# Stacking two half-height coefficient blocks of a fused Fourier-mixing and SwiGLU kernel in the 128 partitions, on one Trainium2 core

## The chip, the cores and the metric

The kernel runs on one core of one Trainium2 chip. The metric is the device time of one execution in microseconds (us). The profile's span is about 2 us shorter than the device time of the same execution. PE is TensorE, PEld its weight loads, DVE VectorE, ACT ScalarE, POOL GpSimd, SP the queue that issues most DMAs.

## The reference

```python
def _attn_ref(x):                        # x: 8 x 3008 x 256, float32
    X = np.fft.fft(x, axis=1)
    X = np.fft.fft(X, axis=2)
    return X.real.astype(np.float32)

def _moe_ref(x, w_gate, w_val, w_out):   # 24064 tokens, 256 -> 1536 -> 256
    g = x @ w_gate
    silu = g * (1.0 / (1.0 + np.exp(-g)))
    val = x @ w_val
    return (silu * val @ w_out).astype(np.float32)
```

## The kernel before

The real part of the Fourier transform has mirror symmetries. The kernel folds each batch's 3008 rows down to one eighth, 188 for the odd sums and 188 for the even sums, multiplies by cosine and sine tables on TensorE, and merges the 256-point transform along the features into the weights. Each 188 are one chunk of 128 rows ("A", the long chunk) and one short chunk ("C") of 60 rows, to which, for the even sums, the row for input row 0 is added. Two batches share the 128 partitions of a short chunk, one in each half.

Each batch has two transform jobs: one for the outputs 4i and 4i+2 (`part == 0`, "4i/4i+2 job"), one for 4i+1 (`part == 1`, "4i+1 job"). A job runs twice, once for each of two operands of the feed-forward part (`eo`, called halves here: `eo=0` fills `Pt`, `eo=1` fills `Qt`), and each half has an odd sum in a PSUM buffer of pool `v` and an even sum in one of pool `g`. ACT copies the odd sum to SBUF (`od`), DVE then adds and subtracts the two into `Pt` or `Qt`. The rest is the feed-forward network: 24 tiles of up to 512 columns, each in 12 units of 128 hidden features. A job is issued between two units, and the units use the same PSUM pools of three buffers each.

```python
psG = ctx.enter_context(tc.tile_pool(name="psG", bufs=3, space=bass.MemoryType.PSUM))
psV = ctx.enter_context(tc.tile_pool(name="psV", bufs=3, space=bass.MemoryType.PSUM))
psO = ctx.enter_context(tc.tile_pool(name="psO", bufs=2, space=bass.MemoryType.PSUM))
# ...
def blocks(b, q):
    p0 = 64 * (b % 2)
    return [(0, slice(0, P), *coef_a(b)), (1, slice(p0, p0 + 64) if b else slice(0, P), *coef_c(b))]

def row0(b, q, ps):
    for ch, r, CE, BB in blocks(b, q):
        for kind, cols in ((0, slice(0, GH + 1)), (1, slice(GH + 1, NCE))):
            nc.tensor.matmul(ps[0:1, cols], CE[r, q, 0, kind, P:P + 1], Tab[r, ch, q, 0, cols],
                             start=False, stop=True, skip_group_check=True)

def transform(b, part, eos, given=None):
    # ...
    for q, pool, nm in ((0, psV, "v"), (1, psG, "g")):
        # ... ps = one buffer for each eo, blk = blocks(b, q)
        for j, (ch, r, CE, BB) in enumerate(blk):
            tab = Tab[r, ch, q]
            for eo in eos:
                for kind in range(2):
                    if part == 0:
                        cols = slice(0, GH + 1) if kind == 0 else slice(GH + 1, NCE)
                        l, r_ = CE[r, q, eo, kind, 0:P], tab[:, eo, cols]
                    else:
                        cols = slice(0, G)
                        l = BB[r, q, eo, kind, 0:P]
                        r_ = tab[:, (eo + kind) % 2, NOO:NTAB]
                    nc.tensor.matmul(ps[eo][:, cols], l, r_, ...)
        if part == 0 and 1 in eos and not given:
            row0(b, q, ps[1])
        for eo in eos:
            if q == 0:
                ods[eo] = odp.tile([P, NCE], F32, name="od")
                nc.scalar.copy(ods[eo][:, 0:n], ps[eo][:, 0:n])
            else:
                ev[eo] = ps[eo]
    # ... DVE: Pt or Qt pieces = ev + od or ev - od

def whole_part(b, part):
    transform(b, part, (0,))
    transform(b, part, (1,))
# ... in the loop over units, after part_a(u) and part_b(prev):
        if i in job_at:
            whole_part(*job_at[i])
```

## Time and profile before

| | before |
|---|---|
| device time, median of 4 runs | 673.07 us (672.6 to 673.18) |
| PE, DVE, ACT, POOL busy share of the span | 98%, 82%, 65%, 63% |
| one 4i/4i+2 job, first matmul to the next unit's first | 3.245 us (first half 1.16) |
| one 4i+1 job, the same | 3.376 us (first half 1.68) |

The page of the kernel before, its span, its first line of busy times (us, share of the span, number of instructions) and the chain of waits, that is the chain of work that ended last, by engine and by line of the kernel:

```profile
span 670.8 us, 12888 instructions
...
PE 656.5 (98%) x4269; PEld 411.6 (61%) x4336; DVE 549.4 (82%) x957; ACT 433.5 (65%) x764; POOL 423.8 (63%) x455
...
PE 94%; DVE 2%; DMA 2%; issue 1%; POOL 1%; ACT 0%; DVEq 0%; ACTq 0%; POOLq 0%
PE o L683 37%; PE g L723 16%; PE v L723 14%; PE g L753 9%; PE v L755 5%; PE v L765 4%; PE g L573 3%; PE v L573 3%; DMA W<-in_moe_w_val_dram 2%; PE g L862 1%; PE v L549 1%; PE g L549 1%; PE o L434 1%; DVE hp L744 0%; DVE hm L768 0%
```

TensorE bounds it. But "98% busy" does not say how well TensorE is used: a matmul's record includes its pipeline latency, so records overlap. A 512-column matmul has a record of 0.38 us and the next one starts 0.217 us later. The Trainium skill says the same of the metric ("Trainium Kernel Development and Optimization", Performance Expectations: matmul busy time is a bad metric, because matmuls are pipelined). What must be read are the distances between starts, called the pitch here: 0.217 us for 512 columns, 0.108 for 256, 0.159 for 376, 0.081 for 189, where nothing disturbs the stream.

The PE timeline of the kernel before, one 4i+1 job (columns: start, duration, engine, line, operation, out<-in, rows*weight columns, shape of the moving operand, how many merged):

```profile
195.71 0.48 PE L573 MATMUL v<-Tab,BBa 128*128 128x376 bf16 x2
196.12 0.49 PE L573 MATMUL v<-Tab,BBc 64*128 64x376 bf16 x2
196.54 0.49 PE L573 MATMUL g<-Tab,BBa 128*128 128x376 bf16 x2
196.97 0.49 PE L573 MATMUL g<-Tab,BBc 64*128 64x376 bf16 x2
197.39 0.49 PE L573 MATMUL v<-Tab,BBa 128*128 128x376 bf16 x2
197.82 0.49 PE L573 MATMUL v<-Tab,BBc 64*128 64x376 bf16 x2
198.24 0.49 PE L573 MATMUL g<-Tab,BBa 128*128 128x376 bf16 x2
198.66 0.49 PE L573 MATMUL g<-Tab,BBc 64*128 64x376 bf16 x2
199.09 0.39 PE L723 MATMUL g<-Pt,Wp 128*128 128x512 bf16 x1
```

A pair should take 2 x 0.159 = 0.32 us, but pairs start 0.41 to 0.43 us apart. The pairs alternate between 128 rows (`128*128`) and 64 rows (`64*128`). The weight loads of the same stretch show what is late:

```profile
195.60 0.21 PEld L573 LDWEIGHTS <-BBa 128*128 128x128 bf16 x2
196.12 0.11 PEld L573 LDWEIGHTS <-BBc 64*128 64x128 bf16 x2 [0.31 <-issue]
196.54 0.11 PEld L573 LDWEIGHTS <-BBa 128*128 128x128 bf16 x2 [0.31 <-issue]
```

Each line merges the two loads of a pair. The first load for 128 rows started at 195.60, 0.11 us before its matmul and under the one before. The first load after a change of the row count starts only with its own matmul (196.12, 196.54), so it is hidden under nothing. From one matmul's start to the next a change takes about 0.255 us instead of 0.159. How much of this is waiting before the load, and how much the load that nothing hides, the records do not separate.

Two events: in the timeline of ACT the copy of the odd sum in a 4i/4i+2 job that started at 167.94; in the timeline of DVE, for the 4i+1 job above, the last step of the unit before (`hp`).

```profile
168.57 0.47 ACT L581 COPY od<-v 128x377 f32<-128x377 f32 x1 [0.43 <-PE v L573]
```

```profile
196.15 0.68 DVE L763 TENSOR_TENSOR hp<-sp,v 128x512 bf16<-128x512 f32 x1
```

The second half's first `v` matmul of that 4i/4i+2 job started at 169.10, just after the copy's end at 169.04.

### The profile page before, as it was taken

To read this page: it belongs to the slowest core of one execution; us is meant where nothing else is said; L and a number is where in the kernel's file an instruction comes from. 1 tells how busy PE (TensorE), PEld (TensorE's weight loads), DVE (VectorE), ACT (ScalarE), POOL (GpSimd) and SP (SyncE) were. 2 spreads that over 40 slices of the span, in tenths; PEclk is the share of its full clock that TensorE was granted. 3 is DMA by queue.
4 is the path that set the end of the run, shared out by engine and by line. 5 is a ranking of instruction groups with operands and counts; after the bars stand their busy time and mean duration, and the time that the engine had idled before them with its cause. 6 is when DMAs were issued, how large, how long until landed. Compare 5 with 4: busy or idle time off the path is not lost.

```text
span 670.8 us, 12888 instructions
## 1 busy us (share of the span) xinstructions
PE 656.5 (98%) x4269; PEld 411.6 (61%) x4336; DVE 549.4 (82%) x957; ACT 433.5 (65%) x764; POOL 423.8 (63%) x455
## 2 busy tenths in 40 slices
PE   8889999999999999999999999999999999999997
PEld 5446666666656666565665666655665656656676
DVE  8796667888888888888888888888888888889962
ACT  8576566666566576575665666656666657666663
POOL 8895953687676787776675767667576333435510
PEclk9999999999999999999999999999999999999999
DMA  9856355335215213344143111125111011111112
GB/s 217 121 76 124 111 127 136 89 92 143 61 33 136 69 50 107 90 98 104 36 109 97 48 33 48 40 68 129 48 41 41 33 44 36 48 32 48 48 48 72
DMA packets 45564, 52.53 MB, mean 78 GB/s; under 512 B 6290, under 2 KB 33466, under 8 KB 45498
## 3 DMA queue, kind: packets, MB, share of 16 engines
q1 hardware_dynamic: 42314, 49.35, 28.0%
q0 software_dynamic: 3184, 2.36, 3.0%
q8 instruction: 34, 0.56, 0.4%
q14 instruction: 32, 0.26, 0.1%
HBM read 29.39 MB, written 24.65 MB: 81 GB/s over the span
## 4 chain that ended last, share of the span: by engine, by line
PE 94%; DVE 2%; DMA 2%; issue 1%; POOL 1%; ACT 0%; DVEq 0%; ACTq 0%; POOLq 0%
PE o L683 37%; PE g L723 16%; PE v L723 14%; PE g L753 9%; PE v L755 5%; PE v L765 4%; PE g L573 3%; PE v L573 3%; DMA W<-in_moe_w_val_dram 2%; PE g L862 1%; PE v L549 1%; PE g L549 1%; PE o L434 1%; DVE hp L744 0%; DVE hm L768 0%
## 5 line engine op out<-in xcount | busy, mean ns | idle before, releaser
L762 POOL TENSOR_TENSOR hm<-sgv,vv 128x512 bf16<-128x512 f32 (+1 forms) x164 | 208.3, 1271 | 190.2 <-DVE vv L758 180.9
L683 PE MATMUL o<-Wo,hp 128*128 128x256 bf16 (+2 forms) x1140 | 169.7, 273 | 0.0
L683 PE MATMUL o<-Wo,hm 128*128 128x256 bf16 (+2 forms) x1140 | 169.7, 273 | 0.0
L683 PEld LDWEIGHTS <-hp 128*128 128x128 bf16 (+2 forms) x1140 | 112.2, 99 | 69.3
L683 PEld LDWEIGHTS <-hm 128*128 128x128 bf16 (+2 forms) x1140 | 112.0, 98 | 69.2 <-issue 0.2
L733 ACT ACTIVATE sp<-g 128x512 f32<-128x512 f32 (+1 forms) x164 | 98.0, 597 | 73.6 <-PE g L723 48.6
L735 DVE SCALAR_TENSOR_TENSOR es<-bc,w,v 128x512 f32<-128x512 f32 (+1 forms) x164 | 121.8, 743 | 5.9 <-PE v L723 5.1
L758 DVE SCALAR_TENSOR_TENSOR vv<-es,v 128x512 f32<-128x512 f32 (+1 forms) x164 | 112.6, 686 | 13.7 <-PE v L755 10.3
L761 ACT ACTIVATE sgv<-g 128x512 f32<-128x512 f32 (+1 forms) x164 | 98.2, 599 | 39.1 <-PE g L753 39.1
L768 DVE TENSOR_TENSOR hm<-sg,v 128x512 bf16<-128x512 f32 (+2 forms) x124 | 82.3, 663 | 41.7 <-ACT sg L767 32.3
L763 DVE TENSOR_TENSOR hp<-sp,v 128x512 bf16<-128x512 f32 (+1 forms) x164 | 111.3, 679 | 0.0
L723 PE MATMUL v<-Pt,Wp 128*128 128x512 bf16 (+2 forms) x288 | 107.9, 375 | 3.4
L723 PE MATMUL g<-Pt,Wp 128*128 128x512 bf16 (+2 forms) x288 | 108.0, 375 | 0.0
L753 PE MATMUL g<-Qt,Wm 128*128 128x512 bf16 (+2 forms) x288 | 107.9, 375 | 0.0
L744 DVE TENSOR_TENSOR hp<-sg,v 128x512 bf16<-128x512 f32 (+2 forms) x124 | 82.4, 664 | 26.6 <-ACT sg L743 24.8
L743 ACT ACTIVATE sg<-g 128x512 f32<-128x512 f32 (+2 forms) x124 | 71.9, 580 | 36.1 <-PE g L723 26.9
L767 ACT ACTIVATE sg<-g 128x512 f32<-128x512 f32 (+2 forms) x124 | 71.9, 580 | 32.5 <-PE g L753 32.3
L723 PE MATMUL g<-Qt,Wq 128*128 128x512 bf16 (+2 forms) x223 | 83.3, 373 | 0.5 <-DVE Qt L586 0.5
L723 PEld LDWEIGHTS <-Wp 128*128 128x128 bf16 x576 | 56.3, 98 | 40.9 <-issue 4.2
L755 PE MATMUL v<-Qt,Wq 128*128 128x512 bf16 (+1 forms) x164 | 62.1, 378 | 0.0
L689 ACT COPY ev<-o 128x512 f32<-128x512 f32 x90 | 52.8, 587 | 7.9 <-PE o L683 7.0
L723 PEld LDWEIGHTS <-Wq 128*128 128x128 bf16 x412 | 40.3, 98 | 19.9 <-issue 0.3
(165 smaller groups left out, 631.2 us busy)
## 6 DMA issues: line engine op xcount, KB each, us to landing
out_dram<-ev SPq DMA_DIRECT2D x96, 128.0 KB
XA<-in_x_dram SPq DMA_DIRECT2D x32, 256.0 KB
XA<-in_x_dram SPq DMA_DIRECT2D x112, 64.0 KB
XC<-in_x_dram SPq DMA_DIRECT2D x32, 120.0 KB
XC<-in_x_dram SPq DMA_DIRECT2D x105, 32.0 KB
out_dram<-ev SPq DMA_DIRECT2D x12, 120.0 KB
out_dram<-ev SPq DMA_DIRECT2D x10, 112.0 KB
XA<-in_x_dram SPq DMA_DIRECT2D x1, 1024.0 KB
```

Of the source, the lines that this page charges most:

```text
L683: nc.tensor.matmul(ps[:n, j, :], hts[minus][:, f, c:c + n], Wo[:, f, :], start=(f == 0), stop=(f == nF - 1))
L723: nc.tensor.matmul(ps[:, :w], Wt[:, gv, fs], src[:, :w], start=start, stop=stop, skip_group_check=True)
L733: nc.scalar.activation(sg[:, :w], g[:, :w], AF.Silu)
L735: nc.vector.scalar_tensor_tensor(es[:, :w], bc[t][:, :w], w0[:, f:f + 1], v[:, :w], op0=Alu.mult, op1=Alu.add)
L744: nc.vector.tensor_tensor(hts[t][0][:, f, :w], sg[:, :w], v[:, :w], op=Alu.mult)
L753: nc.tensor.matmul(g[:, :w], Wm[:, 0, fs], Qt[:, :w], start=False, stop=True, skip_group_check=True)
L755: nc.tensor.matmul(v[:, :w], Wq[:, 1, fs], Qt[:, :w], start=False, stop=True, skip_group_check=True)
L758: nc.vector.scalar_tensor_tensor(vm[:, w - 1::-1], es[:, :w], 2.0, v[:, :w], op0=Alu.mult, op1=Alu.subtract)
L761: nc.scalar.activation(sm[:, w - 1::-1], g[:, :w], AF.Silu)
L762: nc.gpsimd.tensor_tensor(hts[t][1][:, f, :w], sm[:, :w], vm[:, :w], op=Alu.mult)
L763: nc.vector.tensor_tensor(hts[t][0][:, f, :w], sp[:, :w], v[:, :w], op=Alu.mult)
L768: nc.vector.tensor_tensor(hts[t][1][:, f, w - 1::-1], sg[:, :w], v[:, :w], op=Alu.mult)
```

## The change

Intent: do not let the short chunk run at half height. After POOL has folded a short chunk, small SBUF-to-SBUF DMAs put one batch's two kinds of coefficients (4i and 4i+2, and the two kinds of 4i+1) in the two halves of the partitions of a stack tile `St`. In the 4i/4i+2 job each half must meet only its own columns, so the other half of the table is zero; in the 4i+1 job the table is swapped in the upper half. One matmul of 128 rows then replaces two of 64, for batches 1 to 7. The broadcast row `bc` becomes bf16 and one scratch tile shrinks, to make room.

```diff
+    def spread_c(b, F):
+        for half, b_ in ((0, b), (1, b + 1)) if b > 1 else ((1, b),):
+            for kind in range(2):
+                nc.sync.dma_start(out=stack(b_)[64 * kind:64 * kind + 64, :], in_=F[64 * half:64 * half + 64, kind])
 ...
+    def products(b, part, q, eo):
+        CE, BB = coef_a(b)
+        if part == 0:
+            return ([(CE[:, q, eo, k, 0:P], Tab[:, 0, q, eo, e], e) for k, e in ((0, E0), (1, E1))] +
+                    [(stack_of(b, 0)[:, q, eo, 0:P], Tab[:, 1, q, eo, 0:NCE], slice(0, NCE))])
+        res = [(BB[:, q, eo, k, 0:P], Tab[:, 0, q, (eo + k) % 2, NOO:NTAB], slice(0, G)) for k in range(2)]
+        if b:
+            return res + [(stack_of(b, 1)[:, q, eo, :], Tab[:, 0:2, q, eo, NCE:NCE + GH], slice(0, G))]
 ...   (batch 0 as before; row0 likewise: one stack matmul for two)
+    def halve_tables():
+        nc.gpsimd.memset(Tab[0:64, 1, :, :, GH + 1:NCE], 0.0)
+        nc.gpsimd.memset(Tab[64:P, 1, :, :, 0:GH + 1], 0.0)
+    def odd_table(c, half):
+        r = slice(64 * half, 64 * half + 64)
+        src = Tab[r, 1, :, :, NOO + GH * c:NOO + GH * (c + 1)]
+        nc.vector.tensor_copy(Tab[r, c, :, :, NCE:NCE + GH], src[:, :, ::-1] if half else src)
+    before[17] = before.get(17, []) + [halve_tables]
+    for i in range(4):
+        before[13 + i] = [lambda i=i: odd_table(i // 2, i % 2)]
 ...
-            bc[t] = bcp.tile([P, T], F32, name="bc")
+            bc[t] = bcp.tile([P, T], BF16, name="bc")
```

More of the change, by code (lines that the diff above doesn't have):

```diff
@@ L58 @@
     t0 = [sum(wide[:t]) for t in range(nT)]
+    R2 = 4 * G
     NCE = 2 * GH + 1
@@ L75 @@
     cp = ctx.enter_context(tc.tile_pool(name="coef", bufs=2))
+    fcp = ctx.enter_context(tc.tile_pool(name="fc", bufs=1))
+    stp = ctx.enter_context(tc.tile_pool(name="st", bufs=3))
     pqp = ctx.enter_context(tc.tile_pool(name="pq", bufs=5))
@@ L99 @@
     XC = const.tile([P, 8, 2, D], F32, name="XC")
-    SDf = const.tile([P, 2, 4, D], F32, name="SDf")
+    SDf = const.tile([P, R2 // D + 1, D], F32, name="SDf")
     EOf = const.tile([P, 2, 4, P + 1], F32, name="EOf")
@@ L148, in fold_steps @@
         tt = eng.tensor_tensor
-        F = SDf[r, q]
+        F = SDf[r, 0:4]
         E, O = EOf[r, 0], EOf[r, 1]
@@ L178, in quarter_rows @@
         tt(B_[:, 1, :, 0:1], E[:, 3::-3, P:P + 1], E[:, 1:3, P:P + 1], op=Alu.subtract)
-    coefA, coefC = {}, {}
+    coefA, stacks = {}, {}
+    NE = P + 1
+    ND = NE + P
     def coef_a(b):
@@ L186, in coef_a, with stack, stack_of @@
         return coefA[b]
-    def coef_c(b):
-        p = b if b < 2 else 1 + b // 2
-        if p not in coefC:
-            coefC[p] = (cp.tile([P, 2, 2, 2, P + 1], BF16, name="CEc"),
-                        cp.tile([P, 2, 2, 2, P], BF16, name="BBc"))
-        return coefC[p]
+    def stack(b):
+        if b not in stacks:
+            stacks[b] = stp.tile([P, 4 * ND], BF16, name="St")
+        return stacks[b]
+    def stack_of(b, part):
+        S4 = stack(b).rearrange("p (q e n) -> p q e n", q=2, e=2)
+        return S4[:, :, :, 0:NE] if part == 0 else S4[:, :, :, NE:ND]
+    def spread_c(b, F):
+        for half, b_ in ((0, b), (1, b + 1)) if b > 1 else ((1, b),):
+            for kind in range(2):
+                nc.sync.dma_start(out=stack(b_)[64 * kind:64 * kind + 64, :], in_=F[64 * half:64 * half + 64, kind])
     tmp_ctx = ExitStack()
@@ L334 @@
     CEa, BBa = coef_a(0)
-    CEc, BBc = coef_c(0)
+    CEc = tp.tile([P, 2, 1, 2, 1], BF16, name="CEc")
+    BBc = stack(0)[:, 0:8 * P].rearrange("p (q e k d) -> p q e k d", q=2, e=2, k=2)
     ti = [tp.tile([P, 2, NCE], I32, name=f"t1{ch}") for ch in range(2)]
@@ L403, in heads @@
     def heads(eng, ev, od, CE):
-        eng.tensor_tensor(CE[:, :, 0, 0, P:P + 1], ev, od, op=Alu.add)
-        eng.tensor_tensor(CE[:, :, 0, 1, P:P + 1], ev, od, op=Alu.subtract)
+        eng.tensor_tensor(CE[:, :, 0, 0, -1:], ev, od, op=Alu.add)
+        eng.tensor_tensor(CE[:, :, 0, 1, -1:], ev, od, op=Alu.subtract)
     acc = [[None, None], [None, None]]
@@ L539 @@
     last = (pl[:, w_last:w_last + B], ql[:, w_last:w_last + B])
-    def blocks(b, q):
-        p0 = 64 * (b % 2)
-        return [(0, slice(0, P), *coef_a(b)), (1, slice(p0, p0 + 64) if b else slice(0, P), *coef_c(b))]
+    E0, E1 = slice(0, GH + 1), slice(GH + 1, NCE)
     def row0(b, q, ps):
-        for ch, r, CE, BB in blocks(b, q):
-            for kind, cols in ((0, slice(0, GH + 1)), (1, slice(GH + 1, NCE))):
-                nc.tensor.matmul(ps[0:1, cols], CE[r, q, 0, kind, P:P + 1], Tab[r, ch, q, 0, cols],
-                                 start=False, stop=True, skip_group_check=True)
+        CE = coef_a(b)[0]
+        todo = [(CE[:, q, 0, k, P:P + 1], Tab[:, 0, q, 0, e], e) for k, e in ((0, E0), (1, E1))]
+        if b:
+            todo.append((stack_of(b, 0)[:, q, 0, P:P + 1], Tab[:, 1, q, 0, 0:NCE], slice(0, NCE)))
+        else:
+            todo += [(CEc[:, q, 0, k, 0:1], Tab[:, 1, q, 0, e], e) for k, e in ((0, E0), (1, E1))]
+        for l, r_, cols in todo:
+            nc.tensor.matmul(ps[0:1, cols], l, r_, start=False, stop=True, skip_group_check=True)
+    def products(b, part, q, eo):
[4 more added lines that the diff above has]
+        res = [(BB[:, q, eo, k, 0:P], Tab[:, 0, q, (eo + k) % 2, NOO:NTAB], slice(0, G)) for k in range(2)]
+        if b:
+            return res + [(stack_of(b, 1)[:, q, eo, :], Tab[:, 0:2, q, eo, NCE:NCE + GH], slice(0, G))]
+        return res + [(BBc[:, q, eo, k, :], Tab[:, 1, q, (eo + k) % 2, NOO:NTAB], slice(0, G)) for k in range(2)]
     def transform(b, part, eos, given=None):
@@ L557, in transform @@
                 ps = {eo: given[eo][q] for eo in eos}
-                blk = []
             else:
                 ps = {eo: pool.tile([P, T], F32, name=nm) for eo in eos}
-                blk = blocks(b, q)
-            for j, (ch, r, CE, BB) in enumerate(blk):
-                tab = Tab[r, ch, q]
                 for eo in eos:
-                    for kind in range(2):
-                        if part == 0:
-                            cols = slice(0, GH + 1) if kind == 0 else slice(GH + 1, NCE)
-                            l, r_ = CE[r, q, eo, kind, 0:P], tab[:, eo, cols]
-                        else:
-                            cols = slice(0, G)
-                            l = BB[r, q, eo, kind, 0:P]
-                            r_ = tab[:, (eo + kind) % 2, NOO:NTAB]
-                        nc.tensor.matmul(ps[eo][:, cols], l, r_, start=(j == 0 and kind == 0),
-                                         stop=(j == len(blk) - 1 and kind == 1), skip_group_check=True)
+                    mms = products(b, part, q, eo)
+                    for i, (l, r_, cols) in enumerate(mms):
+                        nc.tensor.matmul(ps[eo][:, cols], l, r_, start=(i == 0), stop=(i == len(mms) - 1),
+                                         skip_group_check=True)
             if part == 0 and 1 in eos and not given:
@@ L790 @@
     act_at = {}
+    spread_at = {}
+    foldC = {}
     def run_loads(n):
@@ L805, in fold_step @@
             else:
-                queue[what] = fold_steps(nc.gpsimd, XC, *coef_c(b), q, slice(64 if b == 1 else 0, P))
+                if q == 0:
+                    foldC[b] = fcp.tile([P, 2, 4 * ND], BF16, name="Fc")
+                F5 = foldC[b].rearrange("p k (q e n) -> p q e k n", q=2, e=2)
+                queue[what] = fold_steps(nc.gpsimd, XC, F5[..., 0:NE], F5[..., NE:ND], q,
+                                         slice(64 if b == 1 else 0, P))
         queue[what].pop(0)()
@@ L809, in fold_step @@
             act_at.setdefault(max(unit + 2, 11), []).append(what)
+        if kind == "C" and q == 1 and j == 5:
+            spread_at[unit + 2] = b
     def load_next(what):
@@ L836, in weight_unit @@
         return [lambda k=k: weights(fc, gv, k) for k in range(2)]
-    raO = SDf.rearrange("p k a d -> p (k a d)")[:, 0:4 * G].rearrange("p (c q n) -> p c q n", c=2, q=2)
+    raO = SDf.rearrange("p a d -> p (a d)")[:, 0:4 * G].rearrange("p (c q n) -> p c q n", c=2, q=2)
     def angles_o(ch):
@@ L884 @@
             load_next(what)
+        if i in spread_at:
+            spread_c(spread_at[i], foldC[spread_at[i]])
         if i in job_at:
```

## The prediction

> **What bounds it now.** TensorE. The profile page has PE 98% busy, DVE 82%, ACT 65%, POOL 63%; the chain of waits is 94% PE; PE waits sum to a few us. Matmuls follow at a fixed pitch in the timeline: 0.217 us for 512 columns, 0.108 for 256, 0.159 for 376, 0.081 for 189. PE time taken out counts, unless a PSUM buffer is not free.
>
> **What the change removes.** For batches 1 to 7 the short chunk's matmuls use 64 of 128 rows: two per product, two per row-0 sum. Stacked, each pair becomes one 128-row matmul. Per batch (timeline, b=1):
> - 4i+1 job: 16 matmuls of 376 columns take 3.38 us to the next unit (16 x 0.159 would be 2.54): each of 8 changes between 128-row and 64-row matmuls has a pitch of 0.25 us: the next weight load starts only when the stream is done. The Trainium skill, "TensorEngine Tiling (Array Packing)", Key Properties, says that changing tiling mode drains the TensorE; the trace agrees, about 0.095 us a change. After: 12 x 0.159 = 1.90. Saves 1.47.
> - 4i/4i+2 job: 3.24 us, 24 matmuls. After: first half 2 x (2 x 0.081 + 0.159) = 0.64; the second adds row 0 and four mode changes (one weight column): 1.67. Total 2.31. Saves 0.93.
> Sum 2.4 us x 7 = 16.8 us of PE (2.5%).
>
> **What it adds.** 14 SBUF-to-SBUF DMAs of 128 KB, issued two units after the fold and needed many units later; four DVE table copies and two POOL memsets in units 13 to 17, where DVE is 64% busy; POOL folds keep count and size (0.64 us a quarter-row step). bc in bf16 leaves ACT and DVE durations about alone. All this I expect off the chain.
>
> **How much is on the path.** PE now reaches the transforms' PSUM buffers sooner than ACT and DVE free them.
> - 4i/4i+2 job: the second half's v takes the bank that ACT's od copy of the first half has read; already now (7 of 7) it starts 0.05 us after that copy. The copy can begin only 0.1 us sooner, so the first half saves about 0.1, not 0.42. The second saves its 0.42. About 0.5 per batch.
> - 4i+1 job: the second half's v waits for DVE's hp of the previous unit, which ends 0.4 to 0.7 us before now, while PE would come 0.74 sooner; the next unit's g waits for DVE's Pt sums. Laid out with the trace's durations, next g starts about 1.0 us sooner instead of 1.47.
> Sum 1.5 x 7 = 10.6 us; the other 6 become PE waits in or just after the transforms.
>
> **Prediction: 662.5 us, range 658.5 to 667.** Faster by over 2% (below 659.7): 0.18. Within 2%: 0.80. Slower by over 2%: 0.02.
>
> **What would show it.** Stack matmuls of 128 rows with 0.16 us pitch, no 0.25 us steps inside the 4i+1 job; that job near 2.35 us and the 4i/4i+2 job near 2.75 including waits; PE waits on od copies, hp and Pt sums that are not there now; stack DMAs landing long before use; DVE busy the same within 3 us; span outside the transforms unchanged.
>
> **What would make it wrong.** Faster: the buffer waits being shorter (then up to 656). Slower: stack DMAs or their waits on the SP queue delaying output stores and x loads; POOL folds slower with the new layout; DVE backlog growing after each transform, since DVE needs about 2.1 us for a split unit against PE's 1.95.

## The result, and the profile after

The changed kernel takes 662.56 us (median of 4 runs, 662.1 to 662.89), against 673.07 of before. The ratio is 0.9845, with a 95% interval of 0.9828 to 0.9862. Ratios here are the mean time of one kernel's fast runs over that of the other's of the same rounds, so not quite the ratio of the medians quoted. By a threshold of 2% that counts as the same; it is 1.5% faster, clear of noise.

The page of the changed kernel, the lines that answer to those shown of before:

```profile
span 661.1 us, 12780 instructions
...
PE 644.8 (98%) x4199; PEld 413.5 (63%) x4266; DVE 550.4 (83%) x961; ACT 433.3 (66%) x764; POOL 425.5 (64%) x457
...
PE 93%; DVE 2%; DMA 1%; ACT 1%; issue 1%; SPq 0%; POOL 0%; DVEq 0%; ACTq 0%
PE o L697 37%; PE g L737 16%; PE v L737 14%; PE g L767 9%; PE v L769 5%; PE v L779 4%; PE v L587 2%; PE g L587 1%; DMA XA<-in_x_dram 1%; PE v L438 1%; PE g L438 1%; DVE Pt L600 1%; PE g L897 1%; DVE hp L758 1%; ACT od L595 1%
```

PE's share of the span is still 98%, so that number shows nothing of a 10 us gain. In the chain, two entries from the transforms are new: DVE's `Pt` sums and ACT's `od` copy, 1% each.

The PE timeline of the changed kernel, the same 4i+1 job:

```profile
194.22 0.48 PE L587 MATMUL v<-Tab,BBa 128*128 128x376 bf16 x2
194.54 0.33 PE L587 MATMUL v<-Tab,St 128*128 128x376 bf16 x1
194.70 0.48 PE L587 MATMUL g<-Tab,BBa 128*128 128x376 bf16 x2
195.02 0.33 PE L587 MATMUL g<-Tab,St 128*128 128x376 bf16 x1
195.40 0.48 PE L587 MATMUL v<-Tab,BBa 128*128 128x376 bf16 x2
195.72 0.32 PE L587 MATMUL v<-Tab,St 128*128 128x376 bf16 x1
195.88 0.48 PE L587 MATMUL g<-Tab,BBa 128*128 128x376 bf16 x2
196.20 0.32 PE L587 MATMUL g<-Tab,St 128*128 128x376 bf16 x1
196.58 0.38 PE L737 MATMUL g<-Pt,Wp 128*128 128x512 bf16 x1
```

Inside a half every matmul now has the undisturbed pitch (0.32 for two, 0.16 for one). Two gaps are left. From the last stack matmul of the first half (195.02) to the second half (195.40) it is 0.38 us instead of 0.16, and from 196.20 to the next unit (196.58) again 0.38. DVE's timeline has their ends:

```profile
194.67 0.68 DVE L777 TENSOR_TENSOR hp<-sp,v 128x512 bf16<-128x512 f32 x1
195.45 1.07 DVE L600 TENSOR_TENSOR Pt<-g,od 128x272 bf16<-128x272 f32 x3
```

`hp` ends at 195.35, and `v` starts at 195.40. The `Pt` sums end at 196.52, and the next unit's `g` starts at 196.58. Of the two waits only the second sets the length of the job: over batches 1 to 7 the second half starts anywhere from 1.18 to 1.37 us after the first (after `hp` in six of them, after the `od` copy in batch 1), yet all seven jobs take 2.352 to 2.354 us, and in all seven the next `g` starts 0.05 us after the last `Pt` sum. The 4i/4i+2 job of the same batch, its end of the first half and start of the second:

```profile
167.29 0.33 PE L587 MATMUL g<-Tab,CEa 128*128 128x189 bf16 x2
167.46 0.32 PE L587 MATMUL g<-Tab,St 128*128 128x377 bf16 x1
168.02 0.33 PE L587 MATMUL v<-Tab,CEa 128*128 128x189 bf16 x2 [0.24 <-ACT od L595]
```

The first half could have ended at 167.62 (167.46 + 0.16), and the second starts at 168.02, when the `od` copy is done. The view of the waits of PE has this once per batch (us in total, times, longest); the kernel before has no such line:

```profile
PE v L587 <- ACT od L595: 1.6, 7, 0.2
```

It gives 1.6 us in all, though 7 starts came 0.40 us late, 2.8 us in all. The idle time of PE counts only what the modelled ends of the matmuls leave uncovered, and the pipeline latency covers the rest. It lists nothing at all for the `Pt` sums, although they held up each 4i+1 job. Such waits have to be read from the pitch.

The job times from the trace, batches 1 to 7 (range over the seven jobs), and the gain of all seven together:

| job | before | after | undisturbed stream, worked out from the pitches | gain |
|---|---|---|---|---|
| 4i/4i+2 | 3.243 to 3.249 us | 2.733 to 2.738 | 2.31 | 3.6 us |
| 4i+1 | 3.374 to 3.377 us | 2.352 to 2.354 | 1.90 | 7.2 us |

Outside the jobs nothing moved: the stretches between two jobs (from batch 2's first job on) take 24.52, 49.03 and 48.81 us in both kernels. The sum of gains is 10.7 us. In the two profiles 0.6 us of it is missing, because the set-up ended later in the second (over the profiles the first matmul of the main loop starts anywhere from 24.9 to 26.6 us), and 0.5 us more, because the end of the program came 0.5 us later after the last store was issued. In all profiles the last store is issued 11.02 us after the start of the last unit's first matmul; the end comes at 14.25 us before, at 14.78 in the changed kernel, at 13.97 with the stack DMAs doubled (e5 below). The cause is open.

### The profile page after: what moved, and what is told of

It is laid out like the page before. It is cut to its first block, busy times and chain, and to the rows that moved or that the text cites. A ratio compares the mean times of both kernels' runs of the same rounds, so it can differ in the third digit from the quotient of the medians.

```text
span 661.1 us, 12780 instructions
## 1 busy us (share of the span) xinstructions
PE 644.8 (98%) x4199; PEld 413.5 (63%) x4266; DVE 550.4 (83%) x961; ACT 433.3 (66%) x764; POOL 425.5 (64%) x457
## 4 chain that ended last, share of the span: by engine, by line
PE 93%; DVE 2%; DMA 1%; ACT 1%; issue 1%; SPq 0%; POOL 0%; DVEq 0%; ACTq 0%
PE o L697 37%; PE g L737 16%; PE v L737 14%; PE g L767 9%; PE v L769 5%; PE v L779 4%; PE v L587 2%; PE g L587 1%; DMA XA<-in_x_dram 1%; PE v L438 1%; PE g L438 1%; DVE Pt L600 1%; PE g L897 1%; DVE hp L758 1%; ACT od L595 1%
## 5 line engine op out<-in xcount | busy, mean ns | idle before, releaser
L749 DVE SCALAR_TENSOR_TENSOR es<-bc,w,v 128x512 f32<-128x512 bf16 (+1 forms) x164 | 121.8, 742 | 5.6 <-PE v L737 5.3
```

The source lines that it names most:

```text
L749: nc.vector.scalar_tensor_tensor(es[:, :w], bc[t][:, :w], w0[:, f:f + 1], v[:, :w], op0=Alu.mult, op1=Alu.add)
```

## The experiments

All versions but e3 and e6, which are wrong, compute the right result. The first four share a chip and the runs of the kernel before (median 673.15 us), the next four too (672.06 us), and the last has its own (672.95 us).

### e1_halves_apart: the changed kernel, the halves of a job in two units

```diff
-        if i in job_at:
-            whole_part(*job_at[i])
+        if i - 1 in job_at:
+            transform(*job_at[i - 1], (1,))
+        if i in job_at:
+            transform(*job_at[i], (0,))
```

> The changed kernel, with the two halves of each transform job issued in two successive units instead of back to back. Theory (about 6 us of the 16.8 us of PE time is lost waiting for PSUM buffers between the halves and after the second): the waits fall into other work, so 656 to 657.5 us, ratio to before 0.975 to 0.977, with each half near its stream time (0.64 and 1.68 us for the 4i/4i+2 job, 0.95 and 0.95 for the 4i+1 job). Rival A (the missing 6 us is in the matmul stream itself, for example weight loads from the stack that cannot be prefetched, or lost elsewhere): 662 to 663 us, as the changed kernel.

Measured: 656.78 us (655.92 to 656.99), ratio 0.9763 (0.9748 to 0.9777). The halves of the 4i/4i+2 jobs take 0.65 and 1.69 us, those of the 4i+1 jobs 0.96 and 0.96; the unit between them takes 1.95 us in batches 2 to 7, as elsewhere. The first half of a 4i+1 job in its PE timeline:

```profile
191.82 0.48 PE L587 MATMUL v<-Tab,BBa 128*128 128x376 bf16 x2
192.14 0.32 PE L587 MATMUL v<-Tab,St 128*128 128x376 bf16 x1
192.30 0.48 PE L587 MATMUL g<-Tab,BBa 128*128 128x376 bf16 x2
192.62 0.33 PE L587 MATMUL g<-Tab,St 128*128 128x376 bf16 x1
192.78 0.38 PE L737 MATMUL g<-Pt,Wp 128*128 128x512 bf16 x1
```

Every start follows at its pitch. So the 6 us that the change did not bring were neither in the matmul stream nor in the added work: they were waits between and after the halves, and the timelines above name the PSUM buffers (e4 and e7 test this). Rival A falls.

### e2_halves_apart_old: the same edit on the kernel before

> The kernel before, with the same separation of the halves. Theory: before the change these jobs barely waited for buffers (0.1 us in each of the seven 4i/4i+2 jobs), so 672 to 673 us, within 0.2% of before. Rival B (placing the halves in different units is worth 6 us to any version, whatever the change): near 667 us.

Measured: 672.16 us (671.6 to 672.52), ratio 0.9991 (0.9974 to 1.0008). The first half of a 4i/4i+2 job went from 1.16 to 1.07 us, all else stayed. The same edit is worth nothing measurable before the change and 6 us after it: the shorter stream made the waits. Rival B falls.

### e3_full_rows: the kernel before, short chunk read at full height, nothing stacked

```diff
-        return [(0, slice(0, P), *coef_a(b)), (1, slice(p0, p0 + 64) if b else slice(0, P), *coef_c(b))]
+        return [(0, slice(0, P), *coef_a(b)), (1, slice(p0, p0 + 64) if b == 1 else slice(0, P), *coef_c(b))]
```

> The kernel before, with nothing stacked, but the short chunk's matmuls of batches 2 to 7 read all 128 rows, so that both batches of a pair are added: the numbers are wrong on purpose, the matmul count and the columns are those of before. Theory (in the 4i/4i+2 job two matmuls of 189 and 188 columns cost as much as one of 377; what goes is the mode change): 4i/4i+2 job 2.73 instead of 3.245 us, 4i+1 job about 2.6 instead of 3.376, over six batches 7.7 us, so 665.4 us, ratio 0.988 to 0.990. Rival C (what counts is fewer matmuls and fewer streamed columns): 673 us, no change.

Measured: 664.58 us (664.25 to 665.93), ratio 0.9885 (0.9869 to 0.9901); the result is wrong. A 4i/4i+2 job takes 2.76 us and a 4i+1 job 2.67, in batches 2 to 7. Lines of the PE timeline of one 4i+1 job, where pairs that started 0.42 us apart now start 0.32 apart:

```profile
194.13 0.48 PE L573 MATMUL v<-Tab,BBa 128*128 128x376 bf16 x2
194.45 0.48 PE L573 MATMUL v<-Tab,BBc 128*128 128x376 bf16 x2
194.77 0.48 PE L573 MATMUL g<-Tab,BBa 128*128 128x376 bf16 x2
```

With the same matmuls and the same columns, 1.15% of the 1.55% is there, from six batches instead of seven. Rival C falls: most of the gain of the change is the mode changes that it removes. In the 4i/4i+2 job stacking saves no columns at all (377 in one matmul instead of 189 and 188), and the time is that of the changed kernel to 0.03 us.

### e4_swap_pools: the changed kernel, second half in the other pools

```diff
-        for q, pool, nm in ((0, psV, "v"), (1, psG, "g")):
+        pools = ((psV, "v"), (psG, "g"))
+        for q in range(2):
+            pool, nm = pools[q if given or 0 in eos else 1 - q]
```

> The changed kernel, with the odd and the even sums of the second half taking their PSUM buffers from each other's pool, so that the second half starts in a buffer that an ACT step freed long ago, and not in the one that the od copy reads. Theory: the first half no longer waits (0.64 us in the 4i/4i+2 job instead of 1.05, 0.95 in the 4i+1 job instead of 1.2), and the next unit's g waits for an ACT copy instead of the Pt sums, so 656 to 658 us, ratio 0.975 to 0.978. Rival A: 662 to 663 us.

Measured: 658.13 us (656.9 to 658.6), ratio 0.9782 (0.9766 to 0.9799), so 4.2 us of the 6 come back (0.9845 to 0.9782, of 673). The second half starts 0.96 us after the first in the 4i+1 job, instead of 1.18 to 1.37. The 4i/4i+2 job takes 2.34 us, as the two halves of e1 together, so it waits no more. What is left stands at the end of the 4i+1 job, in the timelines of PE and ACT:

```profile
194.50 0.48 PE L589 MATMUL v<-Tab,BBa 128*128 128x376 bf16 x2
194.82 0.32 PE L589 MATMUL v<-Tab,St 128*128 128x376 bf16 x1
195.23 0.38 PE L739 MATMUL g<-Pt,Wp 128*128 128x512 bf16 x1
```

```profile
194.70 0.47 ACT L597 COPY od<-g 128x376 f32<-128x376 f32 x1 [0.49 <-PE g L589]
```

The next unit's `g` now waits for the second half's `od` copy (194.70 + 0.47 = 195.17, start 195.23). The job takes 2.16 us instead of 2.35. A different remedy removes the same waits in part and leaves the one that its own buffer order makes: they are waits for named buffers, not a general slowness.

### e5_stack_dma_twice: the changed kernel, each stack DMA issued twice

```diff
-            for kind in range(2):
+            for kind in (0, 0, 1, 1):
```

> The changed kernel, with every stack DMA issued twice (28 instead of 14, 1.8 MB more). Theory (the added work is off the chain): 662 to 663.5 us, ratio 0.984 to 0.986, unchanged. Rival D (part of the missing 6 us is the cost of the added DMAs, through the SP queue or the folds that wait for them): the cost doubles, so 665 us or more.

Measured: 662.05 us (661.08 to 662.06), ratio 0.9844 (0.9829 to 0.9859), and the job times are those of the changed kernel. The added DMAs cost nothing that can be measured. Rival D falls.

### e6_full_rows_apart: full height without stacking, halves apart

The edits of e1 and e3 together on the kernel before.

> The kernel before with nothing stacked, all 128 rows read in batches 2 to 7 (wrong numbers on purpose) and the halves of each job one unit apart: mode changes and buffer waits gone, the number of matmuls and streamed columns kept. Theory: per batch 4i/4i+2 job 0.65 + 1.70 us, 4i+1 job 1.27 + 1.27, a gain of about 1.7 us in each of six batches, so 662 to 663.5 us; the rest down to the 656.8 us of the changed kernel with halves apart is what fewer columns bring (0.64 us per 4i+1 job) and batch 1. Rival C (columns make the gain): above 668 us.

Measured: 662.7 us (661.93 to 662.73), ratio 0.9854 (0.9837 to 0.987). The halves take 0.67 and 1.71 us, and 1.27 and 1.27. Against e1 (ratio 0.9763) 0.9% or 6.1 us are missing. Batch 1, which stays at 64 rows here, makes 2.3 us of it (6.52 us of job time against 4.26), and the columns that stacking saves make most of the rest (0.63 us a batch in the 4i+1 job). e2 and e6 differ in the row count alone, and their halves of batches 2 to 7 add up to 6.52 and 4.92 us a batch. So without buffer waits the mode changes were worth 1.6 us a batch, and the columns 0.63.

### e7_od_twice: the changed kernel, each od copy done twice

```diff
-                    nc.scalar.copy(ods[eo][:, 0:n], ps[eo][:, 0:n])
+                    for _ in range(1 if given else 2):
+                        nc.scalar.copy(ods[eo][:, 0:n], ps[eo][:, 0:n])
```

> The changed kernel, with the od copy of every transform half (not of batch 0's first job) done twice by ACT, so 0.47 us later. Theory (the second half of the 4i/4i+2 job waits for the od copy, and the Pt sums that release the next g of the 4i+1 job follow it): 4i/4i+2 job 2.74 to 3.2 us, 4i+1 job 2.35 to about 2.75, about 6 us in all, so 667.5 to 669.5 us. Rival A (no buffer wait matters): 662.5 us, as ACT is 66% busy.

Measured: 668.24 us (667.65 to 668.47), ratio 0.9938 (0.9924 to 0.9953). The 4i+1 jobs take 2.81 us. Three of the seven 4i/4i+2 jobs take 3.24 us; in their PE timeline the second half now comes 1.56 us after the first:

```profile
302.51 0.32 PE L587 MATMUL g<-Tab,St 128*128 128x377 bf16 x1
303.57 0.33 PE L587 MATMUL v<-Tab,CEa 128*128 128x189 bf16 x2 [0.74 <-ACT od L596]
```

The other four take 2.87 to 2.93, where I had expected 3.2: in them the second half's `v` starts 0.05 us after DVE's `hp` or `hm` instead of the `od` copy, so the pool seems to have handed out another buffer. That the total is as expected all the same is partly luck: the 4i/4i+2 jobs lost 2.2 us in all instead of 3.2, the 4i+1 jobs 3.2 instead of 2.8, and batch 0's job 0.3. A longer ACT step on an engine that is busy two thirds of the time costs time where a wanted buffer hangs on it, and only there.

### e8_od_twice_apart: the same with the halves apart

> The same doubled od copy in the version with the halves apart. Theory: there the od copies release nothing that TensorE wants soon, so at most 1 us over the 656.8 us of that version (0.976 of before), 656.5 to 658 us. If a longer ACT step costs time in itself (rival E), the 6 us come here too: 662 us or more.

Measured: 658.33 us (657.99 to 658.49), ratio 0.9792 (0.9777 to 0.9806): 2.0 us over e1 by the ratios, where at most 1 was expected. The excess lies in the stretch between the halves of the 4i/4i+2 jobs, 2.04 to 2.43 us instead of 1.95 in batches 2 to 7, and in both jobs of batch 1. There a unit's `v` takes the buffer that the doubled copy reads, as its PE timeline says:

```profile
167.23 0.38 PE L738 MATMUL v<-Pt,Wp 128*128 128x512 bf16 x1 [0.31 <-ACT od L596]
```

So the next wait is closer in e1 than I thought. But the longer copy costs a third of the 6.3 us (0.9845 to 0.9938) that it costs in the changed kernel, and where it costs, a buffer hangs on it: it does not cost in itself. Rival E falls.

### e9_row0_together: halves apart, row-0 sums of v and g side by side

```diff
-            if part == 0 and 1 in eos and not given:
-                row0(b, q, ps[1])
+            made[q] = ps
+        if part == 0 and 1 in eos and not given:
+            for q in range(2):
+                row0(b, q, made[q][1])
+        for q in range(2):
+            ps = made[q]
             for eo in eos:        # od copy or even sum, as before
```

> The changed kernel with the halves apart, and the row-0 sums (one weight column) of v and g issued next to each other after both products, so two changes of the array's mode per 4i/4i+2 job instead of four. Theory (a change costs about 0.095 us also where the number of weight columns changes): second half of the 4i/4i+2 job 1.50 us instead of 1.69, over seven jobs 1.3 us, so 655 to 656 us, ratio 0.973 to 0.975, if no buffer wait comes of the later od copy. If only changes of the row count cost: 656.8 us.

Measured: 655.04 us (653.97 to 655.65), ratio 0.9732 (0.9718 to 0.9745). The second half of the 4i/4i+2 job takes 1.49 us instead of 1.69. The trace shows the four row-0 pairs behind each other, with a step only before the first and after the last:

```profile
168.97 0.32 PE L587 MATMUL g<-Tab,St 128*128 128x377 bf16 x1
169.22 0.33 PE L564 MATMUL v<-Tab,CEa 128*1 128x189 bf16 x2
169.38 0.32 PE L564 MATMUL v<-Tab,St 128*1 128x377 bf16 x1
169.54 0.33 PE L564 MATMUL g<-Tab,CEa 128*1 128x189 bf16 x2
169.71 0.32 PE L564 MATMUL g<-Tab,St 128*1 128x377 bf16 x1
169.96 0.39 PE L740 MATMUL g<-Pt,Wp 128*128 128x512 bf16 x1
```

From 168.97 to 169.22 it is 0.25 us instead of 0.16, and from 169.71 to 169.96 again. A change of the weight columns from 128 to 1 costs the same 0.09 us as a change of the rows. This version beats both kernels, by 2.7% and 1.1% (the second from two ratios, measured on two chips), and it is right.

## Why the prediction was right

- The bound (TensorE, read from the pitch and not from the busy share) held: the gain is the sum of the shorter jobs, and all else kept its length.
- The removed stream was sized right. e1, where nothing waits, shows halves of 0.65 and 1.69, and of 0.96 and 0.96 us, against the predicted 0.64 and 1.67, and 0.95 and 0.95. e1 comes to 656.8 us; the prediction gave 656 as the floor if no buffer held TensorE up.
- The Trainium skill says that changing the tiling mode drains TensorE ("TensorEngine Tiling (Array Packing)", Key Properties). The trace is consistent with it, with about 0.095 us a change, and e3 shows that this, and not the idle half of the rows, was the larger part. That a matmul over fewer rows takes as long as one over 128 is in the skill too ("TensorE: Matmul & The Clock Gate", Why this matters for your kernels, for 32 rows); here 64 rows of 376 columns had a pitch of 0.17 us in all 28 pairs, as 128 rows have just after a change; 128 rows in an undisturbed stream have 0.159.
- The part on the path, 10.6 of 16.8 us, was right, and for the stated reason. Predicted were 2.75 and 2.35 us for the two jobs with waits, measured 2.735 and 2.353. The waits are for the `od` copy, `hp` and the `Pt` sums (lines above); e1, e4 and e7 show it by taking the waits away, moving them and lengthening one. Of these, the `od` copy (4i/4i+2) and the `Pt` sums (4i+1) cost the time; the wait for `hp` that the prediction also names is there but costs nothing, as the `Pt` sums end later.
- The added work is off the chain: DVE's four table copies take 0.35 to 0.41 us each, POOL's two memsets 0.73, DVE's busy time grew by 1 us, the folds kept 0.63 to 0.64 us, and e5 shows that the DMAs cost nothing. They were issued 34 us or more before the job that reads them; POOL waited for one of them once, for 7.3 us, and no wait of PE names them. The bf16 `bc` changed nothing for DVE (mean of the `es` step 743 ns before, 742 after).
- One point was wrong: the prediction expected to see the new waits as waits of PE in the profile. The `od` wait is listed at 1.6 of its 2.8 us, the `hp` wait at 0.2 us in one job of seven, the `Pt` wait not at all.
- Not tested: taking the waits away by more PSUM buffers (all 8 buffers of the three pools are in use), and reordering the matmuls of the kernel before so that equal row counts follow each other, which would take away part of the mode changes with right numbers and nothing stacked.

## What to carry to other kernels

Before counting columns, look for the places where consecutive matmuls change their row or column count, and try to group equal shapes: here taking the changes of the row count away, at the price of wrong numbers (e3), was worth most of what a restructuring with DMAs and masked tables brought, and grouping the row-0 sums (e9) 0.2 us a job. When a stretch of matmuls gets shorter, follow each PSUM buffer that it wants next to the engine that frees it; a gain beyond that point needs other matmuls in between, which cost four lines here and brought another 0.8%, or another buffer, which brought 0.6%. Of several such waits, the one that ends last sets the gain. Read such gains and waits from the distance between starts, as busy shares and idle sums hide them behind the pipeline's latency.

## What the Trainium skill lacked or had wrong

- "TensorEngine Tiling (Array Packing)", Key Properties, names the drain at a mode change but gives no price. Here it is about 0.095 us a change, for 128 to 64 rows and back, and also for 128 to 1 weight columns and back.
- "TensorE: Matmul & The Clock Gate", Part 3, The mechanism, says that weight loads overlap running matmuls only when the row groups differ. Here loads for the same 128 rows ran under the matmul before (195.60 for a matmul at 195.71), and the first load after a change of the row count started with its own matmul (196.12). It is the "only" that the trace contradicts: no run here loads rows that the running matmul does not use, and Part 2 of the page does allow a load ahead into a background buffer.
- The same page, Back-to-back issue gap, gives about 131 ns a matmul as the sustained pitch of 512 columns with their own weight loads. Here it is 217 ns; its other formula for a single matmul's gap (N / 2.4 + 2.5 ns) gives 159 and 81 ns for 376 and 189 columns, which is what the stream showed.
- "Perfetto Trace Analysis", Identifying Performance Opportunities, takes repeated bubbles as a possible sign of too little SBUF or PSUM. It does not say that short ones hide under the matmuls' latency: 7 starts that were 0.40 us late (2.8 us) are listed as 1.6 us of idle time here, and the waits for the `Pt` sums as none.
